# A batched decode step of two attention and two dense layers on one core: TensorE's own waits, the start of the output projection, and a shorter LayerNorm

## The chip, the core and the metric

The kernel runs on one core of a Trainium2 chip. The core has a matrix engine (TensorE, PE in the profile; its weight loads are listed apart as PEld), a vector engine (VectorE, DVE), a scalar engine (ScalarE, ACT), GpSimd (POOL) and a queue engine that issues transfers here (SyncE, SP). Transfers between the main memory and the on-chip memory are carried out by 16 DMA engines. Engines run side by side, each through its own instructions in order, and wait for each other on semaphores. The metric is the device time in microseconds (us) of one execution; lower is better.

## The reference

Eight sequences (B = 8) each decode one token. Two layers have the same weights and the same caches; each layer is an attention block and a dense block, both behind a LayerNorm without learned factors, and both added to the residual.

```python
def _A_ref(x, k_cache, v_cache, wq, wo):      # x: (8, 1, 512)
    q = (x @ wq) -> (B, Hq=32, 1, Dh=128)
    k, v = caches (B, Hkv=8, Sk=8192, 128), each head shared by 4 query heads
    p = softmax(q . k * Dh ** -0.5)
    return (p @ v) -> (B, 1, 4096) @ wo
def _B_ref(x, w1, w2):                        # 512 -> 1792 -> 512
    return silu(x @ w1) @ w2
x = x + _A_ref(_layernorm(x), ...)
x = x + _B_ref(_layernorm(x), ...)
x = x + _A_ref(_layernorm(x), ...)
x = x + _B_ref(_layernorm(x), ...)
```

All tensors are bf16. K and V caches are 134 MB each and both layers read them, so the caches are the bulk of the work.

## The kernel before

**Tasks and positions.** A task is one (layer, batch row, K/V head): 128 tasks. The 8192 keys of a task are four granules of 2048 keys; a granule of K or of V is one load of 512 KB into one of 27 slots of `arena`. The main loop runs over positions p, eight per task (`GPT`), two per granule. `make_tasks` orders tasks so that layer 1 of one batch row runs among layer 0 tasks of later rows: a row's layer 1 can begin as soon as its own layer 0, output projection and dense block are done.

**Kept K.** For 20 of the 32 granules of a batch row (`KEEP`), the transposed K stays in its slots from layer 0 to layer 1, so layer 1 loads only V for these (352 K loads and 512 V loads in all). While K of a row is kept, seven slots are left for streaming.

**Loads.** `plan_loads` fixes slot, order and the position after which each load may be issued; `issue_until(p)` issues them from SP in that order. A load waits on SP for the readers of its slot, and everything behind it on SP waits with it. At the start, SP issues 4 K granules, wq, the rest of the first 27 slots, then wo, w1 and w2, then the stream.

**One position.** `emit_t` (L430) transposes 1024 keys of K in a TPp bank, eight matmuls; ScalarE (L436, three of eight) or VectorE (L438) writes them back to the slot. `emit_s` (L461) computes scores of a granule, four matmuls into an SCp bank. 14 positions later (`LP`), `emit_pv` (L534) multiplies by V: eight matmuls per position, all 64 of a task accumulate into one OTp bank. Two calls of `emit_pv` stand next to each other at every odd position. Between them lie the softmax steps of a task (L472 to L521): maximum, its spread over partitions by a matmul (L482), exponent, sums, and the transposes of P (L510). `emit_norm` (L548) writes the attended heads to `at1` or `at2`.

**The chain of a batch row.** When the last layer 0 task of row b is normalised, `chain_of(b)` holds a list of pieces: what is left of the output projection, residual, LayerNorm, w1 in two parts, SiLU, w2 in two parts, residual, LayerNorm, wq in four parts. The main loop takes one or more pieces of the chain per position, so that all are done four positions (`EARLY`) before row b's first layer 1 task. Projections (`project`, L603; `wo_part`, L621) accumulate in the bank MISC; for one row they have 32 columns. Before that, as soon as a head is in `at1`, `add_heads` adds its piece of the output projection, 16 matmuls, when the chain is empty; the first of these is at position 23.

**LayerNorm.** `ln_stages(xv, rx, n)` has three stages; the third (L578 to L590) computes the inverse square root on VectorE from an integer seed and three Newton steps (`NEWTON`), then multiplies. It runs with n = 1 sixteen times (two per chain) and with n = 8 at the beginning and at the end.

**Waits.** `op` records every instruction group with the tiles that it reads and writes. `Sync.acquire` collects the counts that it has to wait for (last writers, and for a write the readers too), and `Sync.wait` (L83 to L90) issues a wait unless this engine already waited for as much:

```python
        key = (eng.engine, tok.sem)
        if self.waited.get(key, 0) >= tok.val:
            return
        eng.wait_ge(tok.sem, tok.val)
```

A group that writes a bank which an earlier group of the same engine wrote waits for that group's count too, on its own engine's semaphore.

Of the kernel before, what the change touches and what calls it, by code (L numbers as in the profile page):

```python
# [10 lines left out]
NEWTON = 3  # L11

GRP = 8
GPT = 8
# [4 lines left out]
PRE = 10  # L19
LP = 14  # L20
EARLY = 4
NTP = 3
NSCP = 2
NPT = 2
# [14 lines left out]
ALU = mybir.AluOpType  # L39
# [21 lines left out]
class Sync:  # L61
# [20 lines left out]

    def wait(self, eng, tok):  # L83
        if tok is None:
            return
        key = (eng.engine, tok.sem)
        if self.waited.get(key, 0) >= tok.val:
            return
        eng.wait_ge(tok.sem, tok.val)
        self.waited[key] = tok.val  # L90
# [116 lines left out]
def _build(ctx, nc, A_x, A_k_cache, A_v_cache, A_wq, A_wo, B_w1, B_w2, out):  # L207
# [13 lines left out]
    kept = set(order[len(order) - KEEP:])  # L221
    tasks = make_tasks(B, HKV, (len(order) - KEEP) // NGRAN)
# [3 lines left out]
    NG = len(tasks) * GPT  # L226

    pe = nc.tensor
    dve = nc.vector
# [6 lines left out]
    def sb(shape, dt, name):  # L236
        _cnt[0] += 1
        return ctx.enter_context(nc.sbuf_tensor(f"{name}_{_cnt[0]}", shape, dt))

    def ps_bank(name, dt=FP32):  # L240
        _cnt[0] += 1
        n = 512 if dt == FP32 else 1024
        return ctx.enter_context(nc.psum_tensor(f"{name}_{_cnt[0]}", [128, n], dt))
# [26 lines left out]
    vr = sb([128, B], FP32, "vr")  # L270
    yr = sb([128, B], FP32, "yr")
    tr = sb([128, B], FP32, "tr")
    s1 = sb([128, B], FP32, "s1")
    s1a = sb([128, B], FP32, "s1a")
    xc = sb([128, KT, B], FP32, "xc")
    sq = sb([128, KT, B], FP32, "sq")
    xnT = sb([128, KT, B], BF16, "xnT")
# [20 lines left out]
    OTp = [ps_bank("OTp") for _ in range(2)]  # L298
    TPp = [ps_bank("TPp", BF16) for _ in range(NTP)]
    MISC = ps_bank("MISC")  # L300
# [8 lines left out]
    def res(name):  # L309
        if name not in R:  # L310
            R[name] = Res(name)
        return R[name]
# [4 lines left out]
    def op(eng, inst_fn, reads=(), writes=()):  # L317
        reads = [res(n) if isinstance(n, str) else n for n in reads]
        writes = [res(n) if isinstance(n, str) else n for n in writes]
        syn.acquire(eng, reads, writes)  # L320
        inst = inst_fn()
        tok = syn.mark(inst, eng)
        syn.release(tok, reads, writes)
        return tok
# [31 lines left out]
    with nc.Block() as block:  # L356

        @block.sync
        def _(sync_eng):
# [9 lines left out]
                reads=["ident"], writes=["ident"],  # L369
            )  # L370
            op(dve, lambda: dve.memset(ones[:, :], 1.0), writes=["ones"])
            for n in range(NQB):
# [6 lines left out]
                reads=["ident"], writes=["hm"],  # L379
            )  # L380
            op(dve, lambda: dve.tensor_reduce(real[:, :], hm[:, :], AX.X, ALU.add), reads=["hm"], writes=["real"])
            for c in range(NQ):
# [3 lines left out]
                    op0=ALU.subtract, op1=ALU.mult),  # L386
                   reads=["hm", "real"], writes=["far"])
# [3 lines left out]
            def issue_until(pos):  # L391
                while queue and queue[0].after <= pos:
                    issue(queue.pop(0))
# [27 lines left out]
            def emit_t(i):  # L421
# [3 lines left out]
                tevacs[0] += 1  # L425
                tb = evacs[0] % NTP
                evacs[0] += 1
# [76 lines left out]
            def emit_pt(ti):  # L504
                pb = ti % NPT
                tb = evacs[0] % NTP
                evacs[0] += 1
# [43 lines left out]
            def ln_stages(xv, rx, n):  # L551

                xcv, sqv, xnv = xc[:, :, 0:n], sq[:, :, 0:n], xnT[:, :, 0:n]

                def first():
                    op(dve, lambda: dve.tensor_reduce(s1[:, 0:n], xv.rearrange("p k b -> p b k"), AX.X, ALU.add),
                       reads=[rx], writes=["s1"])
                    op(pool, lambda: pool.partition_all_reduce(s1a[:, 0:n], s1[:, 0:n], 128, bass.bass_isa.ReduceOp.add),
                       reads=["s1"], writes=["s1a"])

                def second():
                    op(
                        dve,
                        lambda: dve.scalar_tensor_tensor(
                            xcv, s1a[:, 0:n].unsqueeze(1).to_broadcast([128, KT, n]), -1.0 / D, xv,
                            op0=ALU.mult, op1=ALU.add,
                        ),
                        reads=["s1a", rx], writes=["xc"],
                    )
                    op(dve, lambda: dve.tensor_tensor(sqv, xcv, xcv, ALU.mult), reads=["xc"], writes=["sq"])  # L570
                    op(dve, lambda: dve.tensor_reduce(s1[:, 0:n], sqv.rearrange("p k b -> p b k"), AX.X, ALU.add),
                       reads=["sq"], writes=["s1"])
                    op(pool, lambda: pool.partition_all_reduce(s1a[:, 0:n], s1[:, 0:n], 128, bass.bass_isa.ReduceOp.add),
                       reads=["s1"], writes=["s1a"])
                def third():
                    v, y, t = vr[:, 0:n], yr[:, 0:n], tr[:, 0:n]
                    vi, yi = v.bitcast(INT32), y.bitcast(INT32)
                    op(dve, lambda: dve.tensor_scalar(v, s1a[:, 0:n], 1.0 / D, LN_EPS, op0=ALU.mult, op1=ALU.add),  # L578
                       reads=["s1a"], writes=["vr"])
                    op(dve, lambda: dve.tensor_scalar(yi, vi, 1, None, op0=ALU.logical_shift_right),  # L580
                       reads=["vr"], writes=["yr"])
                    op(dve, lambda: dve.tensor_scalar(yi, yi, -1.0, RSQRT_SEED, op0=ALU.mult, op1=ALU.add),
                       reads=["yr"], writes=["yr"])
                    for _n in range(NEWTON):
                        op(dve, lambda: dve.tensor_tensor(t, y, y, ALU.mult), reads=["yr"], writes=["tr"])  # L585
                        op(dve, lambda: dve.scalar_tensor_tensor(t, t, -0.5, v, op0=ALU.mult, op1=ALU.mult),
                           reads=["tr", "vr"], writes=["tr"])
                        op(dve, lambda: dve.scalar_tensor_tensor(y, t, 1.5, y, op0=ALU.add, op1=ALU.mult),  # L588
                           reads=["tr", "yr"], writes=["yr"])
                    op(dve, lambda: dve.tensor_tensor(  # L590
                        xnv, xcv, y.unsqueeze(1).to_broadcast([128, KT, n]), ALU.mult),
                       reads=["xc", "yr"], writes=["xnT"])

                return [first, second, third]
# [102 lines left out]
            heads = [[] for _ in range(B + 1)]  # L697

            def add_heads(b):
# [17 lines left out]
                reads=["P", "ident"], writes=["MISC"],  # L717
            )
            op(dve, lambda: dve.tensor_copy(XT[0][:, :, :], MISC[:, 0:KT * B].rearrange("p (k b) -> p k b", b=B)),
               reads=["MISC"], writes=["XT0"])  # L720
# [12 lines left out]
            turn = [0]  # L733
# [4 lines left out]
            for p in range(NG + LP + GPT + 1):  # L738
                tq = (p + LQ) // GPT
                if (p + LQ) % GPT == 0 and tq < ntask:  # L740
                    layer, b, _g = tasks[tq]
                    if layer == 1 and chain and chain_b[0] == b:
                        while chain:
                            chain.pop(0)()
                    emit_q(tq)
                emit_t_until(p + LT)
                if p % GPG == GPG - 1:
                    if p < NG:
                        emit_s(p)
                    for i in range(p - LP - GPG + 1, p - LP + 1):  # L750
                        if 0 <= i < NG:
                            emit_pv(i)
                ti, ph = p // GPT - 1, p % GPT
                if 0 <= ti < ntask and ph in soft:
                    for f in soft[ph]:
                        f(ti)
                if chain:
                    left = max(1, first1[chain_b[0]] - EARLY - p)
                    for _n in range(-(-len(chain) // left)):
                        chain.pop(0)()  # L760
                elif heads[turn[0]] and not (p < NG and tasks[p // GPT][0] and (tasks[p // GPT][2], 0) in kept
                                             and turn[0] < B):
                    add_heads(turn[0])
                done = p - LP - GPT
                if done >= 0 and done % GPT == 0 and done // GPT < ntask:
                    tj = done // GPT
                    emit_norm(tj)
                    layer, b, _g = tasks[tj]
                    if layer == 0:
                        heads[b].append(_g)  # L770
                    elif b == B - 1:
                        heads[B].append(_g)
                    if layer == 0 and tj == last0[b]:
                        assert not chain and turn[0] == b
                        chain.extend([lambda b=b: add_heads(b)] * (HKV - summed[b]) + chain_of(b))
                        chain_b[0] = b
                        turn[0] = b + 1
                issue_until(p)
# [5 lines left out]
            for f in block_stages([XT[2][:, :, :], XT[1][:, :, :], XT[0][:, :, :]], ["XT2", "XT1", "XT0"], B):  # L784
# [8 lines left out]
                reads=["XT0", "ident"], writes=["MISC"],  # L793
# [33 lines left out]
```

## Time and profile before

| what | value |
|---|---|
| median of 3 runs | 1216.26 us (1214.28 to 1218.24) |
| span of the profiled execution | 1216.1 us |
| TensorE busy (PE), weight loads (PEld) | 1048.9 us (86%), 787.6 us (65%) |
| VectorE, ScalarE, GpSimd busy | 598.4 us (49%), 373.9 us (31%), 70.3 us (6%) |
| DMA | 468.02 MB, mean 385 GB/s |
| PV matmuls L534 | 8192, 387.2 us, 186 ns each |
| transposes L430 | 5632, 403.5 us, 223 ns each |
| mean granted TensorE clock | 0.967 |

The profiled execution has no time of its own beside its span; the span lies 0.2 us under the median. Matmuls overlap, so their mean duration is longer than the distance between two of them; the weight loads, one per matmul, show better when TensorE stands still. The DMA share is the mean busy share of 16 engines and can come out a little above 1. In tables of waits, a row is "engine tile line <- what it waited for: us in total, times, longest us". In the chain of waits each row is a start, a duration and what ran then.

### The profile page before, as it was taken

The page shows a single profiled execution, that of the slowest core. Times are in us where ns is not written, and L with a number is a line of the kernel's source. Part 1 is how long each engine was busy: PE and PEld are TensorE (multiplying, and loading weights), DVE is VectorE, ACT ScalarE, POOL GpSimd, SP SyncE. Part 2 cuts the span into 40 slices and gives each one's busy share as a digit, 9 for nine tenths or more (in the row PEclk, how much of TensorE's full clock was granted, in tenths as well). Part 3 has the DMA queues.
Part 4 walks back from the last instruction along what each step waited for, and adds up shares of the span by engine and source line. Part 5 has one row for each costly group of instructions (what it writes and reads, how often), then busy time and mean ns, then how long its engine had stood idle before and what let it go on. Part 6 is the DMA issues. An engine that isn't in the chain of part 4 may idle for free.

```text
span 1216.1 us, 45620 instructions
## 1 busy us (share of the span) xinstructions
PE 1048.9 (86%) x19960; PEld 787.6 (65%) x19960; DVE 598.4 (49%) x1833; ACT 373.9 (31%) x658; POOL 70.3 (6%) x172
## 2 busy tenths in 40 slices
PE   2798888888988889889998898888988898899995
PEld 2576675667666676667676676667666666667664
DVE  2454554546445554546345654556354554456443
ACT  1233322333133322333133322332233322333231
POOL 0000000000000000000000000000000000000000
PEclk9889999999999899999879999999999999999896
DMA  9999989999999999999999999999999999999994
GB/s 373 385 397 402 393 328 409 408 400 389 365 408 409 355 343 403 408 400 388 390 408 403 383 369 409 408 399 362 376 407 402 389 370 408 408 392 380 394 407 169
DMA packets 131621, 468.02 MB, mean 385 GB/s; under 512 B 13904, under 2 KB 19808, under 8 KB 130912
## 3 DMA queue, kind: packets, MB, share of 16 engines
q1 hardware_dynamic: 131424, 465.12, 98.3%
q8 instruction: 158, 2.59, 0.8%
q14 instruction: 39, 0.32, 0.1%
HBM read 465.05 MB, written 0.01 MB: 382 GB/s over the span
## 4 chain that ended last, share of the span: by engine, by line
DMA 53%; PE 34%; SPq 5%; DVE 5%; issue 2%; POOLq 0%; POOL 0%; ACT 0%; DVEq 0%
DMA arena<-in_A_k_cache_dram 46%; PE OTp L534 11%; PE TPp L430 10%; PE SCp L461 5%; SPq L331 5%; DMA arena<-in_A_v_cache_dram 5%; PE MISC L603 4%; DMA wo<-in_A_wo_dram 2%; DVE arena L438 1%; PE OTp L482 1%; PE MISC L621 1%; PE TPp L510 1%; DVE PT L514 0%; DVE tr L585 0%; DVE yr L588 0%
## 5 line engine op out<-in xcount | busy, mean ns | idle before, releaser
L430 PE MATMUL TPp<-ident,arena 128*128 128x128 bf16 x5632 | 403.5, 223 | 80.2 <-DMA arena<-in_A_k_cache_dram 64.6
L436 ACT COPY arena<-TPp 128x1024 bf16<-128x1024 bf16 x264 | 267.2, 1012 | 603.8 <-PE TPp L430 603.8
L438 DVE COPY arena<-TPp 128x1024 bf16<-128x1024 bf16 x440 | 302.0, 688 | 279.4 <-PE TPp L430 279.1
L534 PE MATMUL OTp<-PT,arena 128*128 128x48 bf16 x8192 | 387.2, 186 | 48.1 <-DMA arena<-in_A_v_cache_dram 9.7
L534 PEld LDWEIGHTS OTp<-PT,arena 128*128 128x128 bf16 x8192 | 277.4, 97 | 226.8 <-PE OTp L534 86.1
L430 PEld LDWEIGHTS TPp<-ident,arena 128*128 128x128 bf16 x5632 | 333.8, 100 | 111.6 <-DMA arena<-in_A_k_cache_dram 92.9
L461 PE MATMUL SCp<-arena,QB 128*32 128x512 bf16 x2048 | 210.7, 401 | 7.2 <-DVE arena L438 5.4
L492 ACT ACTIVATE P<-SCp,shift 128x512 bf16<-128x512 f32 x128 | 88.4, 691 | 176.5 <-PE OTp L534 145.2
L501 POOL PARTITION_ALL_REDUCE ssa<-ssm x128 | 55.4, 433 | 998.4 <-DVE ssm L498 970.1
L514 DVE COPY PT<-TPp 128x256 bf16<-128x256 bf16 x128 | 37.3, 291 | 115.2 <-PE TPp L510 115.2
L485 DVE SCALAR_TENSOR_TENSOR own<-OTp,real,far 128x64 f32<-128x64 f32 x128 | 36.3, 284 | 112.8 <-PE OTp L482 112.4
L461 PEld LDWEIGHTS SCp<-arena,QB 128*32 128x32 bf16 x2048 | 53.2, 94 | 56.3 <-DVE arena L438 6.6
L472 DVE TENSOR_REDUCE rowmax<-SCp 128x1 f32<-128x512 f32 x128 | 86.9, 679 | 1.6 <-PE SCp L461 1.2
L482 PE MATMUL OTp<-spread,ones 128*128 128x64 f32 x256 | 52.4, 288 | 0.3 <-DVE spread L474 0.2
L510 PE MATMUL TPp<-ident,P 128*128 128x128 bf16 x512 | 50.4, 221 | 1.6 <-issue 1.6
L498 DVE TENSOR_SCALAR ssm<-hm,rs 128x4 f32<-128x4 f32 x128 | 28.5, 223 | 36.7 <-ACT P L492 36.7
L621 PE MATMUL MISC<-at,wo 128*128 128x32 bf16 (+1 forms) x1152 | 40.0, 176 | 7.1 <-DMA wo<-in_A_wo_dram 6.8
L482 PEld LDWEIGHTS OTp<-spread,ones 128*128 128x128 f32 x256 | 40.1, 198 | 0.6 <-DVE spread L474 0.6
L621 PEld LDWEIGHTS MISC<-at,wo 128*128 128x128 bf16 x1152 | 34.5, 96 | 7.5 <-DMA wo<-in_A_wo_dram 6.9
L603 PE MATMUL MISC<-xnT,wq 128*128 128x32 bf16 (+1 forms) x1152 | 34.7, 176 | 3.2 <-issue 2.8
L603 PEld LDWEIGHTS MISC<-xnT,wq 128*128 128x128 bf16 x1152 | 32.7, 97 | 3.7 <-issue 3.1
L474 DVE TENSOR_SCALAR spread<-ident,rowmax 128x64 f32<-128x64 bf16 x128 | 32.6, 254 | 4.6
(47 smaller groups left out, 293.7 us busy)
## 6 DMA issues: line engine op xcount, KB each, us to landing
arena<-in_A_v_cache_dram SPq DMA_DIRECT2D x512, 512.0 KB, 10.8
arena<-in_A_k_cache_dram SPq DMA_DIRECT2D x352, 512.0 KB, 14.9
wq<-in_A_wq_dram SPq DMA_DIRECT2D x1, 4096.0 KB, 16.5
wo<-in_A_wo_dram SPq DMA_DIRECT2D x1, 4096.0 KB, 25.9
w<-in_B_w_dram SPq DMA_DIRECT2D x2, 1792.0 KB, 22.6
P<-in_A_x_dram SPq DMA_DIRECT2D x1, 8.0 KB
out_dram<-P SPq DMA_DIRECT2D x1, 8.0 KB
```

The source lines that it names most:

```text
L331: eng.dma_start(out_ap, in_ap).then_inc(counter.sem, 16)
L430: lambda c=c: pe.transpose(tpv[:, c, :], chunk(slot, h * GRP + c), ident[:, :])
L436: op(act, lambda: act.copy(dst, TPp[tb][:, :]), reads=[f"TP{tb}"], writes=[r_half(slot, h)])
L438: op(dve, lambda: dve.tensor_copy(dst, TPp[tb][:, :]), reads=[f"TP{tb}"], writes=[r_half(slot, h)])
L461: lambda c=c: pe.matmul(SCp[bank][c * QUAD:(c + 1) * QUAD, :], QB[qn][:, NGRAN - 1 - k:NGRAN - 1 - k + QUAD], ARENA[:, slot * SLOT + c * K ...
L472: op(dve, lambda: dve.tensor_reduce(rowmax[:, :], SCp[bank][:, :], AX.X, ALU.max), reads=[f"SC{bank}"], writes=["rowmax"])
L482: mm_group([lambda: pe.matmul(every, ones[:, :], spread[:, :], start=True, stop=True)], reads=["ones", "spread"], writes=[f"OT{ob}"])
L492: op(act, lambda: act.activation(P[:, :], SCp[bank][:, :], ACT.Exp, bias=shift[:, 0:1], scale=SM_SCALE, accum_out=rs[st][:, :]), reads=[f" ...
L510: lambda c=c: pe.transpose(tpv[:, c, :], P[:, c * 128:(c + 1) * 128], ident[:, :])
L534: lambda c=c, cc=cc: pe.matmul(otp, chunk(slot, h * GRP + c), pv[:, cc % CPB, cc // CPB % NQ, k, :].unsqueeze(2).to_broadcast([128, REP, P ...
L603: lambda o=o, k=k: pe.matmul(MISC[:, o * n:o * n + w], w_sb[:, k, o * 128:(o + 1) * 128], rhs_of(k).to_broadcast([128, w]) if n == 1 else ...
L621: lambda o=o, h=h: pe.matmul(MISC[:, o * w:(o + 1) * w], wo_sb[:, h, o * 128:(o + 1) * 128], rhs_of(h).to_broadcast([128, w]) if n == 1 el ...
```

## The change

Three edits. `Sync.wait` returns at once when the waiting engine is TensorE and the semaphore is TensorE's own. `add_heads` outside a chain is allowed only from position 36 (`WO_FROM`). For n = 1, the third stage of LayerNorm leaves the Newton steps unnormalised: each step is two instructions in place of three, and the factor that gathers is a constant that the last product takes out.

```diff
+WO_FROM = 36
 ...
     def wait(self, eng, tok):
         if tok is None:
             return
+        if eng is self.nc.tensor and tok.sem is self.eng_sem[eng.engine]:
+            return
 ...
+                    if n == 1:
+                        scale = 1.0
+                        for _n in range(NEWTON):
+                            op(dve, lambda: dve.tensor_scalar(t, y, y, v, op0=ALU.mult, op1=ALU.mult),
+                               reads=["yr", "vr"], writes=["tr"])
+                            op(dve, lambda: dve.tensor_scalar(y, t, -3.0 * scale ** 2, y, op0=ALU.add, op1=ALU.mult),
+                               reads=["tr", "yr"], writes=["yr"])
+                            scale *= -2.0 * scale ** 2
+                        op(dve, lambda: dve.tensor_scalar(xnv, xcv, y, 1.0 / scale, op0=ALU.mult, op1=ALU.mult),
+                           reads=["xc", "yr"], writes=["xnT"])
+                        return
                     for _n in range(NEWTON):
                         op(dve, lambda: dve.tensor_tensor(t, y, y, ALU.mult), reads=["yr"], writes=["tr"])
 ...
-                elif heads[turn[0]] and not (p < NG and tasks[p // GPT][0] and (tasks[p // GPT][2], 0) in kept
+                elif p >= WO_FROM and heads[turn[0]] and not (p < NG and tasks[p // GPT][0] and (tasks[p // GPT][2], 0) in kept
                                              and turn[0] < B):
                     add_heads(turn[0])
```

In the program that comes out, TensorE's instructions stand in the same order except for the first two pieces of the output projection, which move from positions 23 and 31 to 36 and 37. VectorE has 48 instructions fewer. Nothing changes on ScalarE, GpSimd and SP.

## The prediction

> **What bounds the kernel now.** I read the page first (span, slices, queue, chain), then the busy time by stretches of 10 us, the chain of waits in order of time, and the tables of waits.
>
> ```profile
> span 1216.1 us, 45620 instructions
> GB/s 373 385 397 402 393 328 409 408 400 389 365 408 409 355 343 403 408 400 388 390 408 403 383 369 409 408 399 362 376 407 402 389 370 408 408 392 380 394 407 169
> q1 hardware_dynamic: 131424, 465.12, 98.3%
> DMA 53%; PE 34%; SPq 5%; DVE 5%; issue 2%; POOLq 0%; POOL 0%; ACT 0%; DVEq 0%
> ```
>
> The run streams 465.12 MB, and many slices sit at 407 to 409 GB/s: that is the ceiling. All bytes at 408 GB/s take 1140 us; with some 8 us before the stream is full and 20 us after the last V load lands (1195.6 us), nothing that leaves the bytes alone gets below about 1168 us. What other engines can win lies in the slices under the ceiling (328, 365, 355 and 343, 369 ...), which return about once per batch row. One of these places, in stretches of 10 us (columns: PE, weight loads, DVE, ACT, POOL busy, clock, DMA share, GB/s):
>
> ```profile
> 690.00:700.00 10.00, 8.27 (x180) 6.57 (x179) 7.40 (x32) 3.69 (x7) 1.24 (x3) 1.00 1.03 408
> 700.00:710.00 10.00, 9.76 (x214) 7.91 (x214) 6.44 (x24) 4.10 (x7) 1.21 (x3) 1.00 1.01 372
> 710.00:720.00 10.00, 9.16 (x231) 7.69 (x230) 5.64 (x17) 2.53 (x5) 0.16 (x1) 1.00 0.96 365
> 720.00:730.00 10.00, 9.27 (x184) 6.13 (x185) 3.82 (x15) 2.02 (x7) 0.72 (x2) 1.00 1.00 370
> 730.00:740.00 10.00, 9.22 (x180) 5.98 (x178) 4.10 (x17) 1.81 (x7) 0.86 (x2) 1.00 1.03 412
> ```
>
> and the chain of waits through it (start, us, what):
>
> ```profile
> 693.02 0.17 DVE tr L585
> ...
> 694.84 0.70 DVE arena L438
> ...
> 705.22 5.09 DMA arena<-in_A_k_cache_dram
> ...
> 712.59 0.32 PE OTp L534 x8
> 712.90 0.04 issue
> 712.95 0.37 PE OTp L534 x8
> ...
> 731.02 14.66 DMA arena<-in_A_k_cache_dram
> ```
>
> From 710 to 731 us the chain is TensorE almost without a break: the PV pieces (L534), the last projections of the chain of one batch row (L603, L621), transposes and scores. TensorE is the bound there and the DMA queue runs thin; at 731 the chain is DMA again. So the kernel is bound by DMA, except for some 30 us around each of eight batch rows.
>
> **Part 1: TensorE's own semaphore.** Instructions of TensorE wait 924 times on TensorE's own count in the program before (378 as separate instructions, 546 on a matmul), never in the one after. Most cost nothing, since the awaited group ended long ago. The exception is the second of two PV groups on one OTp bank:
>
> ```profile
> PEld OTp L534 <- PE OTp L534: 86.1, 512, 0.2
> PE MISC L621 <- DMA wo<-in_A_wo_dram: 6.8, 1, 6.8
> ```
>
> 512 waits, 86.1 us, 0.17 us each: eight weight loads take 0.27, then the second eight wait until the first eight have drained. In the chain a pair takes 0.32 + 0.05 + 0.37 = 0.74 at most and mostly 0.69 to the next transposes; sixteen without a break should take 2 x 0.27 = 0.54. I take 0.16 us per pair. Groups that TensorE does not hold on itself already follow each other without a gap (L621 to L430: 16 matmuls in 0.40), so nothing else on TensorE should step into the place of this wait.
>
> Which pairs count? At 402 GB/s or more the time goes to the DMA wait behind them: the cover is the stream itself, and it is gone only where TensorE is late. I went through the chain in 10 us steps and counted the L534 groups in stretches under 402 GB/s, ramp and tail left out: 218 groups, 109 pairs, some 14 for each batch row (the place shown has 14 from 691 to 731). 109 x 0.16 = 17.4 us. The bounds: nothing, if the stream cannot take more there; at most the whole deficit against 408 GB/s in these stretches, 46 us summed, of which roughly 37 us lie at the eight batch rows. Each row saves 2.2 us and lacks between 2.7 and 8.7 us, so the ceiling bites little. I take 17.4.
>
> After the last load, five PV pairs are on the chain between 1195.7 and 1202: 5 x 0.16 = 0.8 us. All of it counts, since only dependent work follows.
>
> SP's queue issues the loads and waits for TensorE (its waits on L461 and L534 sum to 257 and 201 us): these come earlier with TensorE, in the same order, and no wait is added on any queue.
>
> **Part 2: WO_FROM = 36.** Only batch row 0 is touched: its first two wo pieces (16 matmuls, 0.40 us each) leave positions 23 and 31 and run at positions 36 and 37. No DMA moves. The 6.8 us wait for wo at 54.6 us (second row above) goes, and with it about 5 us at half clock behind it. But the DMA share is 1.10 and 1.03 while TensorE stands: the stream is not starved, only the wo load is late in a queue that is full. The first loads behind the weights are issued at 57 and 65 us; TensorE, 7 to 9 us earlier, runs through what the first 27 slots hold and then waits for those loads instead. At 84 us before is already back to waiting for K. I cost it at nothing. Bounds: the first 90 us after the ramp lack 2.5 us against 408 GB/s in all, so +2.5 if the stream did gain; as much lost if two more pieces and a new cold clock hit it. By position 36 wo has landed (61.4 us against roughly 68 or later).
>
> **Part 3: LayerNorm of one row.** Three Newton steps of three instructions become three of two, sixteen times (48 fewer), and where the old ones had plain tensor operands, each new one, the closing product too, reads one column per partition as a scalar (y or v), three of them two. VectorE runs in order: the stage holds the transposes' evacuation (L438) behind it, and scores wait for that.
>
> ```profile
> L498 DVE TENSOR_SCALAR ssm<-hm,rs 128x4 f32<-128x4 f32 x128 | 28.5, 223 | 36.7 <-ACT P L492 36.7
> L585 DVE TENSOR_TENSOR tr<-yr 128x1 f32<-128x1 f32 x48 | 7.6, 159 | 1.7
> ```
>
> Before: nine at 0.159 + 0.036 between them = 1.76 us, and the closing product 0.18. The new kind is nearest to L498 (a column operand, 0.223): six at 0.26 = 1.55, and the closing one 0.05 dearer. Saved 0.15 us. Bounds: at the old price 0.59 saved; if a second column costs again what the first does (0.223 less 0.159, three times), 0.04 lost. On the chain this stage shows once per batch row (693.02 is one; the second LayerNorm of a row is covered by TensorE): 8 x 0.15 = 1.2 us, between -0.3 and +4.7. The tail's LayerNorm has eight columns and stays as it was.
>
> Here the Trainium skill says otherwise. The page "VectorE: DVE Perf Modes", section "The TRN2 errata", has an SBUF instruction pay a fixed cost plus its elements, whatever its operands; by it the new ones cost what the old cost and the sum would be 3.5 us lower. The rows differ (0.223 at four elements with a column, 0.159 to 0.178 at one to four without), so I go by the rows.
>
> **The sum.** 17.4 + 0.8 + 0 + 1.2 = 19.4 us off the profiled 1216.1: 1196.7. The span is 0.2 us under the median of 1216.26, so the forecast is 1197 us, 1.6% faster. A difference of 0.3% (3.6 us) is about what can be told from no change.
>
> **Rivals.** (a) The stream hides most of it. In the stretches just before the deficits (262 to 284 us) loads come back in loops of 6 us from issue to landing with TensorE waiting; if the deficits are of this kind too, a faster TensorE only waits longer. Against it: 710 to 731 has no DMA wait in the chain. Part 1 then gives a third, 6 us: 1209.
> (b) More than the sum. A thin queue refills earlier, so the next stretch starts with a lead; then most of the 37 us at the batch rows could go. With 75% of it: 28 us, 1187.
> (c) Slower: the clock. TensorE falls to half clock after short gaps:
>
> ```profile
> 397.53 0.81 PE L534 MATMUL OTp<-PT,arena 128*128 128x48 bf16 x16 [1.41 <-DMA arena<-in_A_v_cache_dram]
> 400.00:405.00 5.00, 4.94 (x54) 3.54 (x54) 2.02 (x5) 2.34 (x5) 0.43 (x1) 0.50 0.82 275
> ```
>
> After a gap of 1.41 us the next 5 us run at 0.50 and the stream falls to 275 GB/s, 1.6 us lost there. A faster TensorE waits longer for each load at the mouth of the dense stretches (0.38 us at 443.7 now; three or four pairs more would make it about 1.0). If that tips the clock at all eight rows, twice each, at 1.3 to 1.6 us, 16 x 1.5 = 24 us eat the gain: 1221. It decides from about 13 such falls. Against it: a gap of 1.60 at 440.9 left the clock at 1.00. The page "TensorE: Matmul & The Clock Gate" of the Trainium skill (Part 1) asks for an idle window of about 3.4 us before the clock drops; by that none of these gaps would count and (c) would be out. The trace has drops after 1.2 to 1.4 us, so (c) stays in.
> (d) No change: the drain is paid anyway, because the second PV group is held by accumulation into the same bank. Then 1215. Against it: projections accumulate into one bank at 25 ns a matmul.
>
> **Chances.** The sum (1190 to 1204) 0.62; (a) 0.15; (b) 0.11; (c) 0.07; (d) 0.05. The range leaves out the far half of (b), (c) and (d): 1184 to 1212. Faster by over 0.3%: the sum, (b) and nearly all of (a), 0.86; within 0.3%: (d) and the edges of (a) and (c), 0.07; slower 0.07.
>
> **What the profile will show.** The row "L534 waits for L534" gone, and TensorE's L534 pairs 0.54 us apart from what follows; the slices that held 328 to 370 GB/s now at 375 to 400, with 407 to 409 unchanged; the wait for wo gone and a K wait of several us between 60 and 75 us in its place; new LayerNorm instructions at 0.22. I am wrong if the low slices stay low with longer DMA waits in front (a), or if the clock row has more digits below 9 (c).

## The result, and the profile after

The changed kernel takes 1205.74 us (median of 4 runs, 1205.11 to 1207.62) against 1217.25 us for the kernel before in the same comparison: a ratio of 0.9918, with a 95% interval from 0.989 to 0.9945. It is faster, by 0.8% and not by the 1.6% that was forecast. The profiled execution has a span of 1203.4 us and took 1205.11 us, so 1.7 us lie around its span, where the prediction had taken 0.2.

The page of the profile after, the same four lines as before:

```profile
span 1203.4 us, 45191 instructions
GB/s 372 385 396 403 397 374 408 407 403 392 388 408 407 386 366 409 408 403 385 384 407 406 392 368 408 408 394 379 402 408 401 385 373 408 408 387 369 401 408 164
q1 hardware_dynamic: 131424, 465.12, 98.9%
DMA 66%; PE 24%; DVE 5%; issue 3%; SPq 2%; POOL 0%; POOLq 0%; ACT 0%; DVEq 0%
```

The ceiling of 408 GB/s is untouched. The deepest slices have risen (328 to 374, 343 to 366), but the low places are still there, once per batch row, and the chain of waits is more DMA (66% for 53%) and less TensorE (24% for 34%). Summed over stretches of 10 us from 70 us to the end of the stream, what is missing against 408 GB/s fell from 47.0 to 34.2 us: 12.8 us, which is the difference of the two spans (12.7). So in these two profiles the whole change lies where the prediction looked for it, in the stream's low places, and about a quarter of what was missing has been won.

The stretches around the end of one row's chain (the same row that the prediction showed, some 10 us earlier here; columns PE, weight loads, DVE, ACT, POOL busy, clock, DMA share, GB/s), and the chain of waits through it:

```profile
690.00:700.00 10.00, 8.37 (x211) 7.25 (x208) 7.42 (x28) 3.80 (x6) 1.21 (x3) 1.00 0.99 375
700.00:710.00 10.00, 9.02 (x242) 7.55 (x239) 4.83 (x14) 2.90 (x5) 0.44 (x1) 1.00 0.92 338
710.00:720.00 10.00, 8.63 (x201) 5.94 (x197) 4.56 (x17) 1.73 (x6) 0.87 (x2) 1.00 0.98 379
720.00:730.00 10.00, 8.27 (x156) 5.47 (x152) 3.20 (x13) 1.73 (x6) 0.80 (x2) 0.83 1.03 410
```

```profile
693.48 5.71 DMA arena<-in_A_k_cache_dram
...
701.43 0.51 PE OTp L537 x16
...
706.52 0.80 PE MISC L617 x32
...
711.55 0.27 PE OTp L485 x2
...
712.09 7.74 DMA arena<-in_A_v_cache_dram
719.83 15.84 DMA arena<-in_A_k_cache_dram
```

A pair of PV groups is now one piece of 0.51 us on the chain, where it had been 0.32 + 0.05 + 0.37 and mostly 0.69 to the next instruction: 0.18 us saved each time. But the chain leaves TensorE at 712 us, just behind the last query projections, for a V load. Before, it stayed with TensorE through the kept tasks until the next K load, at 731 us. In this row the three low stretches are no better than they were.

More places that the prediction named, in rows of the profile after: the timeline of TensorE behind the wo load, the stretch of 5 us there (columns as above), and the groups of the new LayerNorm (busy us, mean ns, idle before; the first, with constants only, is there for comparison).

```profile
72.76 0.82 PE L537 MATMUL OTp<-PT,arena 128*128 128x48 bf16 x16 [10.70 <-DMA arena<-in_A_v_cache_dram]
```

```profile
70.00:75.00 5.00, 1.79 (x25) 1.67 (x26) 0.00 (x0) 0.00 (x0) 0.00 (x0) 0.50 1.04 408
```

```profile
L581 DVE TENSOR_SCALAR vr<-s1a 128x1 f32<-128x1 f32 x16 | 2.4, 151 | 0.2
L590 DVE TENSOR_SCALAR tr<-yr,vr 128x1 f32<-128x1 f32 x48 | 13.1, 273 | 1.7
L592 DVE TENSOR_SCALAR yr<-tr,yr 128x1 f32<-128x1 f32 x48 | 10.3, 214 | 1.7
L595 DVE TENSOR_SCALAR xnT<-xc,yr 128x4 bf16<-128x4 f32 x16 | 3.8, 236 | 0.6
```

The stall of 6.8 us for wo is gone, and one of 10.7 us for the first V load behind the weights has come, with the clock at half after it. LayerNorm has 48 instructions fewer, but the six new ones are busy for as long as the nine old ones: 3 x (0.273 + 0.214) = 1.46 us for 9 x 0.159 = 1.43.

### The profile page after: what moved, and what is told of

The parts are those of the page before. It is cut to its first block, busy times and chain, and to the rows that moved or that the text cites. A ratio compares the mean times of both kernels' runs of the same rounds, so it can differ in the third digit from the quotient of the medians.

```text
span 1203.4 us, 45191 instructions
## 1 busy us (share of the span) xinstructions
PE 964.9 (80%) x19960; PEld 751.2 (62%) x19960; DVE 601.3 (50%) x1785; ACT 373.9 (31%) x658; POOL 70.4 (6%) x172
## 4 chain that ended last, share of the span: by engine, by line
DMA 66%; PE 24%; DVE 5%; issue 3%; SPq 2%; POOL 0%; POOLq 0%; ACT 0%; DVEq 0%
DMA arena<-in_A_k_cache_dram 58%; PE TPp L433 10%; DMA arena<-in_A_v_cache_dram 8%; PE MISC L617 4%; PE OTp L537 4%; PE SCp L464 3%; SPq L334 2%; DVE arena L441 1%; PE OTp L485 1%; DVE tr L590 1%; PE MISC L635 1%; PE TPp L513 0%; DVE yr L592 0%; DVE rowmax L475 0%; DVE own L488 0%
## 5 line engine op out<-in xcount | busy, mean ns | idle before, releaser
L537 PEld LDWEIGHTS OTp<-PT,arena 128*128 128x128 bf16 x8192 | 242.8, 96 | 181.3 <-DMA arena<-in_A_v_cache_dram 139.0
L537 PE MATMUL OTp<-PT,arena 128*128 128x48 bf16 x8192 | 297.9, 185 | 54.5 <-DMA arena<-in_A_v_cache_dram 46.9
```

Source lines behind the costliest of these rows:

```text
L537: lambda c=c, cc=cc: pe.matmul(otp, chunk(slot, h * GRP + c), pv[:, cc % CPB, cc // CPB % NQ, k, :].unsqueeze(2).to_broadcast([128, REP, P ...
```

## The experiments

All ratios are against the kernel before, run on the same chip beside it. One measure is used throughout: what the stream lacks against 408 GB/s (length x (408 - GB/s) / 408), summed over the eight batch rows in three phases, by the end of a row's query projection. "Loops" is from 60 to 25 us ahead of it, "chain" from 25 to 5 us ahead, "after" from 5 us ahead to 20 us behind. The last takes in the last wq pieces and the first kept layer 1 tasks. Each value comes from one profiled execution, which can lie several us from its kernel's median (1219.75 for 1213.30 us where only the kept tasks skip, 1187.50 for 1182.79 with a quarter of the projections), and kernels that take nearly the same time differ by up to 4 us in a phase: the kernel with the later output projection alone has 8.9, 11.8 and 19.2 where before has 12.8, 11.6 and 21.4.

| kernel | ratio and interval | loops, us | chain, us | after, us |
|---|---|---|---|---|
| before | 1 | 12.8 | 11.6 | 21.4 |
| the whole change | 0.9918 (0.9890 to 0.9945) | 9.2 | 9.7 | 13.9 |
| own waits skipped only within the chain | 0.9957 (0.9935 to 0.9979) | 8.0 | 11.7 | 15.9 |
| own waits skipped only in the kept tasks | 0.9985 (0.9962 to 1.0008) | 13.5 | 12.8 | 21.6 |
| 27 slots, w2 left out | 0.9891 (0.9855 to 0.9927) | 8.2 | 9.1 | 17.5 |
| 30 slots, w2 left out | 0.9700 (0.9671 to 0.9729) | 0.3 | 2.0 | 10.4 |
| the same, with own waits | 0.9765 (0.9742 to 0.9788) | 0.3 | 3.9 | 16.2 |
| a quarter of the chain's projections | 0.9744 (0.9720 to 0.9768) | 9.5 | 4.5 | 1.9 |
| the same, with own waits | 0.9737 (0.9712 to 0.9762) | 6.3 | 3.5 | 2.0 |
| 19 granules kept | 0.9930 (0.9910 to 0.9949) | 2.5 | 6.9 | 15.3 |
| one more wait per pair than before | 1.0146 (1.0106 to 1.0185) | 10.8 | 19.8 | 23.0 |

### The three edits apart

Four kernels keep one or two of the edits and undo the others. The diffs against the changed kernel of the three undoings are:

```diff
-        if eng is self.nc.tensor and tok.sem is self.eng_sem[eng.engine]:
-            return
```

```diff
-WO_FROM = 36
+WO_FROM = 0
```

```diff
-                    if n == 1:
-                        scale = 1.0
...
-                        return
```

The first run undoes the last two of them, the second the first two, the third the first and the last, the fourth the last alone.

> Only the first edit: TensorE skips waits on its own semaphore; the output projection starts at position 23 and LayerNorm is as before. Theory S (the prediction's sum, with its size capped by something that does not depend on TensorE): nearly the whole change, 10 to 13 us under before, ratio 0.989 to 0.992. Theory C (the clock: the gain came because TensorE no longer stands 6.8 us for wo and does not fall to half clock at three places): the wait for wo stays, so part of the gain is missing, 5 to 8 us, ratio 0.993 to 0.996, and the clock row shows falls near 160, 400 and 845 us as before.

> Only the third edit, LayerNorm of one row in two instructions per Newton step. From the profile after: 3 x (0.273 + 0.214) + 6 x 0.036 = 1.68 us against 1.76 before, the closing product 0.06 dearer: 0.02 us saved per LayerNorm, 16 times. Theories S and C both: within 1 us of before, ratio 0.999 to 1.001. The prediction's row for it (0.15 us saved on the chain per batch row) would be 1.2 us, at the edge of what can be seen.

> Only the second edit, the output projection's pieces from position 36. Theory S: the stall moves to the next late load, 0, ratio 0.999 to 1.001. Theory C: the missing stall for wo is worth 2 to 5 us, ratio 0.996 to 0.998.

> First and second edit, LayerNorm as before. Theory S and C: as the whole change, ratio 0.990 to 0.993 (1204 to 1207 us); if the new LayerNorm costs more on the chain than it saves, this is 1 to 2 us faster than the whole change.

Measured: own waits alone 0.9928 (0.9901 to 0.9954), 1207.12 us; LayerNorm alone 1.0003 (0.9985 to 1.0020); the later start of the output projection alone 0.9990 (0.9974 to 1.0007); the first two together 0.9920 (0.9898 to 0.9942). The first edit is the change: 0.72% of 1215.5 us is 8.8 us. The other two cannot be told from nothing. The clock theory does not hold. It gave the later output projection 2 to 5 us, and 1.2 us were measured (0.9 lost to 3.2 won). The ratio of the first edit alone lies between the two theories and does not decide, and neither does its profile, for the profiled execution is the slowest of its eight (1214.72 us). But the mean granted clock of its eight runs is 0.9735, and that of the 25 runs of before beside them 0.9730: the gain came at the same clock. So the mechanism was right, and its size is what needs explaining: 512 pairs are 0.18 us shorter, 92 us of TensorE, and 8.8 us come out.

### Which pairs count

```diff
+        self.skip = False
...
-        if eng is self.nc.tensor and tok.sem is self.eng_sem[eng.engine]:
+        if self.skip and eng is self.nc.tensor and tok.sem is self.eng_sem[eng.engine]:
...
+                dense = bool(chain) or p < NG and tasks[p // GPT][0] == 1 and (tasks[p // GPT][2], 0) in kept
+                syn.skip = dense == True
```

In the second kernel the last line ends on False.

> The whole change, but TensorE skips its own waits only in the dense places: while the chain of a batch row runs, and in layer 1 tasks whose K is kept (248 of the 512 pairs of PV groups). Theory S (only pairs where TensorE is late count, as the prediction has it): all of the gain is here, ratio 0.990 to 0.993 against before. Rival L (a lead: pairs elsewhere count as well, because TensorE then arrives earlier at the dense place with more loads landed): about half, ratio 0.994 to 0.997.

> The complement: TensorE skips its own waits everywhere but in the dense places (264 of 512 pairs). Theory S: nothing but the 0 to 2 us of the other two edits, ratio 0.998 to 1.000. Rival L: about half of the gain, ratio 0.994 to 0.997.

Measured: 0.9933 (0.9908 to 0.9958) where the waits are skipped in the dense places only, and 0.9972 (0.9953 to 0.9992) where they are skipped only elsewhere. In us of 1215: 8.1 and 3.4. Most of it is in the dense places, as the prediction had it, but not all, so part of the rival is true: a pair elsewhere gives some lead. The dense places miss the prediction's size too: 248 pairs at 0.18 us would be 45 us of TensorE there, of which 18% comes out.

Two further kernels divide the dense places: skipping only while a chain is not empty, or only in kept tasks once it is empty.

```diff
+                syn.skip = bool(chain)
```

```diff
+                syn.skip = not chain and p < NG and tasks[p // GPT][0] == 1 and (tasks[p // GPT][2], 0) in kept
```

> The whole change, with TensorE skipping its own waits only while the chain of a batch row is not empty (88 of 512 pairs). Theory E (early: what TensorE is behind when the kept layer 1 tasks begin sets the loss, so pairs within the chain give their full 0.18 us, 88 x 0.18 = 16 us at most): 5 to 8 us under before, ratio 0.993 to 0.996. Theory W (while: the pairs in the kept tasks are the ones that count): 0 to 3 us, ratio 0.9975 to 1.000.

> The whole change, with TensorE skipping its own waits only in layer 1 tasks whose K is kept, once the chain is empty (160 of 512 pairs). Theory E: 0 to 3 us under before, ratio 0.9975 to 1.000. Theory W: 5 to 8 us, ratio 0.993 to 0.996.

Measured: 0.9957 (0.9935 to 0.9979) within the chain, 0.9985 (0.9962 to 1.0008) in the kept tasks. So 88 pairs give 5.2 us (2.6 to 7.9), 0.06 us each, and 160 pairs give 1.8 us or nothing (at most 4.6), 0.01 us each. The 264 others gave 3.4 us (1.0 to 5.7), 0.013 us each. All these kernels have the other two edits as well, which by their own runs lose 0.4 and win 1.2 us, neither clear of nothing, so the small values may be theirs; the 0.06 us stands out even so. The table points the same way, with one execution each: skipping within the chain lowers what is missing behind it ("after": 15.9 for 21.4 us), skipping in the kept tasks does not (21.6). What TensorE is behind when the kept tasks begin decides; the pairs in these tasks hardly count, although the chain of waits before ran through them. That chain shows why. Over the phase "after" of the eight rows it holds 135 us of TensorE and 50 us of DMA before. With the waits skipped in the kept tasks alone it holds 86 and 101: 49 us of TensorE went off it, and loads took their place.

### Is it the chain that makes TensorE late?

```diff
-                    for k in range(kparts):
+                    for k in range(kparts if n > 1 else max(1, kparts // 4)):
...
-                                start=(k == 0), stop=(k == kparts - 1),
+                                start=(k == 0), stop=(k == (kparts if n > 1 else max(1, kparts // 4)) - 1),
```

The second run below takes the skipped wait out again as well. Theory Q has it that what remains is too few loads in flight and not a late TensorE; the next section tests it.

> The whole change with three quarters of the matmuls in the chain's w1, w2 and wq projections left out (fewer steps of the contraction; one row only). TensorE has about 182 x 0.025 = 4.5 us less for each of eight batch rows, all in the dense places. If a late TensorE is what remains: 15 to 30 us under the whole change, ratio 0.968 to 0.980. Theory Q: 3 to 10 us, ratio 0.984 to 0.990.

> The run with a quarter of the chain's w1, w2 and wq matmuls (the rest left out), but TensorE waits on its own semaphore again. If the wait costs only where the chain makes TensorE late: 0 to 3 us above that run, ratio 0.974 to 0.977 against before. If it costs the same everywhere: 8 to 10 us above it, ratio 0.981 to 0.983.

Measured: 0.9744 (0.9720 to 0.9768) with a quarter of the chain's projections, and 0.9737 (0.9712 to 0.9762) with TensorE's own waits put back into it. The slices of the second on its page, and its row in the table of waits:

```profile
GB/s 372 385 396 399 401 408 407 408 396 390 406 408 408 395 402 408 408 404 401 399 406 406 394 400 408 408 404 398 406 407 404 398 404 407 406 400 399 406 408 159
```

```profile
PEld OTp L535 <- PE OTp L535: 85.5, 512, 0.2
```

This is the clearest result. All 512 waits are there, 85.5 us of them, as in the kernel before; with the chain light they cost nothing that can be seen (the two intervals leave room for some 3 us), and no slice under 394 GB/s is left between 60 us and the tail except one of 390. And 182 matmuls of 25 ns less per row, 36 us of TensorE in all, bring 21 us against the whole change by the ratios: more than half comes out. What is missing behind the chain goes with it ("after": 1.9 for 13.9 us), so this work stands where TensorE falls behind. The theory that few loads in flight are all that is left had 3 to 10 us for it.

### Slots

The base of two runs leaves w2 out, which makes room; the two then have 30 slots. The last run changes one constant of the changed kernel.

```diff
-    w2_sb = sb([128, FT, D], BF16, "w2")
+    w2_sb = w1_sb[:, :, :].rearrange("p k f -> p (k f)").rearrange("p (f d) -> p f d", d=D)
...
-                dma(sp, w2_sb[:, :, :], B_w2.rearrange("(ft p) d -> p ft d", p=128), wsem["w2"], writes=["w2"])
...
-                    project(w2_sb, "w2", KT, FT, lambda k: hsT[:, k * n:(k + 1) * n], "hsT", n, parts),
+                    project(w2_sb, "w1", KT, FT, lambda k: hsT[:, k * n:(k + 1) * n], "hsT", n, parts),
```

```diff
-NSLOT = 27
+NSLOT = 30
```

```diff
-KEEP = 20
+KEEP = 19
```

> The whole change, with w2 left out: its tile is w1's (so the second dense projection multiplies by w1's numbers) and its load is not made. A base for the next run. One load of 1.8 MB less is 4.5 us at 408 GB/s: 1201 us, ratio 0.987 to 0.990.

> The run before it with the room used: 30 slots in place of 27, so ten and not seven slots stream while 20 hold K. Theory Q (what is left of the deficit under 408 GB/s, some 34 us, is too few loads in flight, not a late TensorE; this also capped the gain): 12 to 25 us under the run with 27 slots, ratio 0.968 to 0.980 against before. Theory T (what is left is TensorE still late, more PV waits or not): up to 5 us under it, ratio 0.983 to 0.989, since more slots only let TensorE be late for longer.

> As the run with 30 slots (w2 left out, its products from w1's numbers), but TensorE waits on its own semaphore again. Theory Q (few loads in flight cap what TensorE can win; with ten streaming slots the stream bridges a late TensorE): the wait costs 0 to 4 us here, ratio 0.970 to 0.973 against before. If it is not a matter of slots and the wait costs what it cost with 27 slots, 8 to 10 us: ratio 0.977 to 0.979.

> The whole change, with 19 granules of K kept per batch row in place of 20: eight loads more (8 x 1.285 = 10.3 us at 408 GB/s) and eight streaming slots instead of seven; nothing is left out. Theory Q: the eighth slot gives back 8 to 14 us, so -4 to +2 us against the whole change, ratio 0.988 to 0.993. If slots do not matter: 10 us slower than the whole change, ratio 1.000.

Measured: 0.9891 (0.9855 to 0.9927) for the base, 1202.37 us; 0.9700 (0.9671 to 0.9729) with 30 slots, 1179.13 us; 0.9765 (0.9742 to 0.9788) with 30 slots and own waits, 1185.95 us; 0.9930 (0.9910 to 0.9949) with 19 kept. The page with 30 slots:

```profile
GB/s 374 393 399 407 408 390 409 408 408 407 380 407 407 408 399 407 409 407 395 380 407 407 408 394 408 408 407 403 398 408 408 404 392 408 408 408 395 395 407 165
```

Three more slots bring 23 us: the loops vanish (8.2 to 0.3 us), the chain phase nearly (9.1 to 2.0), and "after" falls from 17.5 to 10.4. So seven streaming slots are the second cause of the low places. But they do not cap what the wait is worth: with 30 slots it costs 6.8 us by the medians and 7.9 by the ratios, within the interval of what it costs with 27 (5.6 to 12.0), where the theory had 0 to 4. That part of the theory fell. Nineteen kept granules bear the first part out: eight loads more, 10.3 us of stream, and no loss against the whole change. No run has more slots and a light chain together.

### How the cost grows

```diff
-                mm_group(steps, reads=[r_half(slot, h), f"PT{pb}"], writes=[f"OT{ob}"])
+                for part in ([steps[:4], steps[4:]] if i % 2 else [steps]):
+                    mm_group(part, reads=[r_half(slot, h), f"PT{pb}"], writes=[f"OT{ob}"])
```

> The kernel before, with the second PV group of each pair cut in two, so that a pair has two waits on TensorE's own semaphore and not one (512 waits of 0.17 us more; nothing is left out). Proportional: 9 us slower than before, ratio 1.006 to 1.009. Growing (the stream hides part of the first wait, and less of the next): 14 us or more, ratio 1.011 or more.

Measured: 1.0146 (1.0106 to 1.0185), 17.7 us slower. Its row of own waits:

```profile
PEld OTp L534 <- PE OTp L534: 170.8, 1024, 0.2
```

Twice the waiting, 85 us more, costs 17.7 us more (12.9 to 22.5); the first 86 us cost 8.8 (5.6 to 12.0). The cost grows, as it would if the stream hid most of the first wait of a pair and less of the second. What the extra group costs beside its wait is not separated.

### Half of the PV matmuls

```diff
                 for c in range(GRP):
                     cc = (i % GPT) * GRP + c
+                    if c % 2 and cc != NCH - 1:
+                        continue
```

> The whole change with half of the PV matmuls left out (every second one of each group), so that a pair of PV groups takes TensorE some 0.25 us instead of 0.51. All loads stay. If a late TensorE is what remains under 408 GB/s: 14 pairs x 8 rows x 0.26 = 29 us, limited by the 34 us that are missing: at least 15 us under the whole change, ratio 0.975 to 0.980. Theory Q: 3 to 8 us under it, ratio 0.985 to 0.990.

Measured: 0.9870 (0.9845 to 0.9895), 1200.28 us, 5.8 us under the whole change by the ratios. Taken alone this agrees with the theory of few loads in flight, but it can't decide, for the mean granted clock fell to 0.897 (0.976 in the whole change). In stretches of 5 us of this kernel:

```profile
715.00:720.00 5.00, 3.31 (x56) 2.00 (x55) 2.08 (x8) 0.87 (x3) 0.86 (x2) 0.96 1.00 390
720.00:725.00 5.00, 4.29 (x45) 2.05 (x43) 1.89 (x7) 0.72 (x3) 0.00 (x0) 0.50 1.02 415
725.00:730.00 5.00, 4.90 (x59) 2.69 (x55) 2.12 (x8) 0.74 (x4) 0.43 (x1) 0.50 1.02 410
```

Part of what the lighter TensorE gained may have been paid back at half clock; how much is open.

## Why the prediction was right in kind and half in size

**Own waits: right price, wrong count.** The price was 0.16 us a pair and is 0.18. The step that failed is the count: "109 pairs ... 109 x 0.16 = 17.4 us", with "the ceiling bites little". The edit alone gave 8.8 us (5.6 to 12.0 by its interval). Every pair that the chain of waits showed in a stretch under 402 GB/s was taken to give its full price. The chain shows the longest path, not by how much it is the longest. Behind the kept tasks' TensorE work a path through loads was nearly as long: in the profile after, the chain leaves TensorE at 712 us for a V load, and the pairs behind it are worth 0.01 us each. Over the phase "after" of the eight rows the chain lost 60 us of TensorE (135 to 75) and took up 64 us of DMA (50 to 114), while the span is 12.7 us shorter. Within the chain of a row a pair gives 0.06 us, a third of its price. The deficit summed against 408 GB/s (37 us at the batch rows) was taken as room for TensorE to fill; part of it belongs to the seven streaming slots and to the chain's own projections, which no shorter wait touches.

**The rivals.** The outcome lies between the sum and rival (a), "the stream hides most of it". (a) looked at the loops of 6 us ahead of the chain; whether these hide anything can't be told (12.8 us missing before, 9.2 in the whole change, and 8.9 with the waits kept and only the output projection later). It is in the dense places that the stream hides most. (b) did not happen: the lead from pairs elsewhere, 3.4 us, does not compound. (c) did not happen: the wait at the mouth of the dense stretch grew, and by more than foreseen (1.63 us ahead of 699.2 us, where about 1.0 was expected), but the clock stayed at 1.00 there, and the mean granted clock of the profiled execution is 0.976 for 0.967. (d) is out: the pair is 0.51 us.

**WO_FROM: right.** Nothing in the time (0.9990, 0.9974 to 1.0007); the stall moved to the next late load. It was a V load and 10.7 us at 72.8, where a K load and several us by 75 had been forecast. The DMA share was 1.04 to 1.09 from 60 to 75 us: the queue stayed full while TensorE stood.

**LayerNorm: the far bound was nearly right.** Forecast 0.15 us saved each time and 1.2 us in all, with a bound of 0.04 lost if a second column costs what the first does. It does: 0.214 us with one column, 0.273 with two, 0.159 in the old instructions without. Six new instructions take 3 x (0.273 + 0.214) + 6 x 0.036 = 1.68 us for 1.76, the closing product 0.06 more, so 0.02 us is saved; alone the edit measures 1.0003. The page "VectorE: DVE Perf Modes" of the Trainium skill, section "The TRN2 errata", gives a fixed cost plus the elements and no term for a column operand; by it 0.59 us would have been saved each time, and these rows do not agree with it.

**The tail: another path than forecast.** Five pairs were to stand behind the last load, each 0.16 us shorter. In the profile after, the V load that the chain follows last lands at 1188.27 us, and one pair stands behind it; before, it landed at 1195.64 with five. So it is in all nine profiles of kernels that skip the wait there, while seven of the nine that keep it have five pairs or more. From that landing to the end it is 15.1 us for 20.5, but the stream runs thin ahead of it (115 GB/s in the last 4 us, for 406). In all, the 12.8 us in the stream leave nothing of the 12.7 for the tail, and 0.8 us is below what the runs resolve.

No version here that does all the work beats both kernels clearly: the first two edits without the new LayerNorm, and 19 kept granules, measure like the whole change.

## What to carry to other kernels

A piece on the chain of waits is worth its price only up to the length of the next path, so a saving taken off in many places is to be counted by the place where the engine falls behind, and with a guess for the path behind it; here a third came out in the right place and almost nothing elsewhere. Before taking small waits off an engine that shares a bound with a stream, take out, as a test, the dense work that makes it late: here a test with a quarter of that work showed both that the waits then cost nothing and where the larger gain lies. Fewer instructions are not less time: operands read as columns per partition made six instructions as long as nine.

## What the runs showed that was not expected

The clock falls without a long gap. In the kernel with half of the PV matmuls the clock was 0.50 from 720 to 730 us; in the 10 us ahead of it TensorE never stood for more than 0.73 us at a time, and its weight loads were busy for 2.0 of 5 us. In the kernel before, a gap of 1.6 us at 440.9 had left the clock at 1.00. The page "TensorE: Matmul & The Clock Gate" of the Trainium skill (Part 1) speaks of an idle window of about 3.4 us; these rows do not agree with it, for here the clock fell with no gap near that. How thin the work is over 5 us does not decide either. In the same kernel a gap of 2.20 us, with weight loads as thin (2.01 of 5 us), left the clock at 1.00:

```profile
943.21 1.07 PE L433 MATMUL TPp<-ident,arena 128*128 128x128 bf16 x16 [2.20 <-DMA arena<-in_A_k_cache_dram]
```

```profile
940.00:945.00 5.00, 2.80 (x58) 2.01 (x56) 1.69 (x6) 1.70 (x2) 0.43 (x1) 1.00 1.02 399
945.00:950.00 5.00, 3.74 (x70) 2.87 (x67) 3.54 (x13) 1.40 (x3) 0.79 (x2) 1.00 0.99 365
```

What decides is open.

A scalar operand read per partition costs VectorE about 0.06 us each on tiles of one column: 0.151 us with constants, 0.214 with one, 0.273 with two.
